# Attention with the queries on the partitions, in plain float32, ahead of two MoE layers

## The chip, the cores and the metric

The kernel runs on one core of a Trainium2 chip. The metric is the device time of one execution in microseconds (us). A difference of about 0.2% (2 us) is what a measurement of this kernel can tell from none.

## What is computed

The reference is a causal attention joined with a linear memory, and two feed-forward layers behind it. B = 4, H = 8, S = 576, D = 64, all in float32:

```python
scores = scale * np.matmul(q, k.transpose(0, 1, 3, 2))
...
a = np.exp(scores)
a /= a.sum(-1, keepdims=True) + 1e-09
local = np.matmul(a, v)
...
mem_ret = np.einsum('bhsd,bhde->bhse', q_p, M_prev)
mem_norm = np.einsum('bhsd,bhd->bhs', q_p, z_prev)[..., None] + 1e-06
mem_out = mem_ret / mem_norm
...
return (g * mem_out + (1 - g) * local).astype(np.float32)
```

Here q_p = phi(q), which is max(q, 0) + exp(min(q, 0)), and g is a sigmoid per head. The result, as x with 2304 rows of 512, goes through g(x @ w_in) @ w_out with a squared ReLU (d_ff = 2048), and then through a gated layer with d_ff = 1536.

## The kernel before

Every product is made at about float32 accuracy out of float32r parts: an operand is split into a rounded high part ("hi", ScalarE) and the rest ("lo", VectorE or GpSimd), and three products hi·hi, lo·hi and hi·lo are summed in PSUM.

The work is written as tasks with an engine, an assumed duration, an urgency from the table TUNE, the data they read and write, and the buffers that they take. The class Plan (line 41) runs a list scheduler over the tasks when the program is built, and its result is the order of each engine's instructions, which is then fixed. Buffer counts are in the table `slots`: PSUM has four banks of tag "s", one double bank of tag "w" and two banks of tag "h" in the first stage.

There are three stages. **The first** is 16 attention jobs (4 batches by 4 pairs of heads) and, between and behind them, the 128 chunks of h = x @ w_in (`h_mm`, line 313; 12 matmuls of 256 or 320 columns each). A chunk needs x of its batch and window (queries 0 to 255, or 256 to 575), so the first chunk needs the four jobs of batch 0. The weights w_in are decoded from 64-bit words (lines 248 to 275), 16 tiles with three VectorE steps each. **The second** is y = g @ w_out (`y_mm`, line 1048) and **the third** the gated layer (products m, line 1294, and the output o, line 1397).

One job, before:
- K and Q are transposed on TensorE (`transposed`, 5 + 5 blocks, line 416) and split into hi and lo (lines 480 to 504). The scores of five tiles of 128 queries are summed with the queries on the partitions (lines 626 and 652). VectorE adds the mask and finds the maximum (line 606), ScalarE takes the exponential and its row sum (line 668), and GpSimd multiplies P by the inverse sum (line 684).
- phi(q) is made with the queries on the partitions, normalised by z on VectorE and GpSimd (lines 519 to 551), transposed (`ft`) and split into hi and lo, stacked (lines 424 to 430). GpSimd splits V and M_prev (lines 404 to 407, 590 to 593).
- P is transposed in 25 blocks of 128x128 (`trans`, line 753), and each group is split: hi by ScalarE (line 776), lo by VectorE (line 780). The product (`pv`, lines 806 to 811) has V's hi and lo side by side as the stationary operand and the transposed P as the moving one, 64 to 320 columns, so that x comes out already transposed. The two halves are joined by ScalarE (line 830) and VectorE (line 834) in XB, and once a batch is whole it is split into hi and lo (lines 891 and 895).

Of the kernel before, what the change touches and what calls it, by code (L numbers as in the profile page):

```python
# [20 lines left out]
FB = 1  # L21
# [9 lines left out]
}  # L31
ENG = {"split": "DVE"}
# [118 lines left out]
def attention_moe_kernel(  # L151
# [18 lines left out]
    P = 128  # L170
# [166 lines left out]

    rawq = at.tile([P, NQ, P], F32, name="rawq", bufs=1)
    rawk = at.tile([P, NQ, P], F32, name="rawk", bufs=1)
    rawv = at.tile([P, NQ, P], F32, name="rawv", bufs=1)  # L340

    def zero_raw():


        for e in range(2):
            nc.gpsimd.memset(rawq[e * LAST : (e + 1) * LAST, NQ - 1, (1 - e) * D : (2 - e) * D], 0.0)
        nc.gpsimd.memset(rawk[LAST:, NQ - 1], 0.0)
        nc.gpsimd.memset(rawv[: P - LAST, NQ - 1], 0.0)
# [4 lines left out]
    iom = at.tile([P, NP, NC], F32, name="iom", bufs=1)  # L353

# [9 lines left out]
    def load_consts2():  # L364
        for e in range(2):
            c = slice(e * NQ, e * NQ + NT4)
            nc.vector.tensor_copy(iom[:, :, c], iomg[:, e::2].unsqueeze(2).broadcast_to([P, NP, NT4]))
            r = slice(e * LAST, (e + 1) * LAST)
            nc.vector.tensor_copy(iom[r, :, NT4], iomg[r, e::2])

    def load_raw(j, src, dst, ta):
        b, p, t0, t1 = jobs[j]
        te = min(t1, NQ - 1)
        d4 = dst.rearrange("p t (h d) -> p t h d", h=2)
# [17 lines left out]
    def load_mem(j):  # L392
        b, p = jobs[j][:2]
        h = slice(2 * p, 2 * p + 2)
        raw = T["mraw", j] = at.tile([P, 2, D], F32, tag="mraw", name=f"mraw{j}", bufs=1)
        for i in range(2):
            nc.sync.dma_start(raw[i * D : (i + 1) * D], M_prev[b, h].rearrange("h d e -> d h e"))
        z = T["z", j] = at.tile([P, 2, D], F32, tag="zbc", name=f"zbc{j}", bufs=1)
        nc.sync.dma_start(z, z_prev[b, h].partition_broadcast(P))

    def prep_m(j):
        raw = T.pop(("mraw", j))
        t = T["m", j] = at.tile([P, 2, 2, D], F32R, tag="mst", name=f"mst{j}")
        nc.gpsimd.tensor_scalar(
            out=t[:, :, 0], in0=raw, scalar1=1.0, scalar2=1.0, op0=ALU.mult, op1=ALU.mult
        )
        nc.gpsimd.tensor_tensor(out=t[:, :, 1], in0=raw, in1=t[:, :, 0].bitcast(F32), op=ALU.subtract)
# [14 lines left out]
    def stack_hi(t, ds):  # L422

        nc.scalar.copy(ds[0][:D], t[:D])
        nc.scalar.copy(ds[1][D:], t[D:])

    def stack_lo(t, ds):
        a, c = t[:D], t[D:]
        nc.vector.tensor_tensor(out=ds[0][D:], in0=a, in1=ds[0][:D].bitcast(F32), op=ALU.subtract)
        nc.vector.tensor_tensor(out=ds[1][:D], in0=c, in1=ds[1][D:].bitcast(F32), op=ALU.subtract)  # L430

    engine = {"DVE": nc.vector, "POOL": nc.gpsimd}
    slots = {
        "s": 4, "w": 1, "h": 2, "r": 2, "rawq": 1, "rawk": 1, "rawv": 1, "mem": 1, "mst": 2,
        "QT": 2, "KT": 2, "VHL": 2, "phi": 1, "phit": 1, "nrm": 2, "FS": 2, "P0": 3,
        "P1": 3, "P2": 3, "P3": 3, "P4": 1, "rs0": 2, "rs1": 2, "sums": 2, "PTA": 1, "PTB": 1,
        "PTC": 1, "XB": 1, "x0": 1, f"x{SPLIT}": 1, "raw": 2, "f": FB, "wt": 16,
# [8 lines left out]
    def mm(n):  # L446
        return max(108, 15 + n // 2.35)

# [6 lines left out]
    def plan_load(j):  # L455
# [4 lines left out]
        for src, dst, ta, key, du in (  # L460
            (q, rawq, t0, "rawq", AT["lq"]), (k, rawk, 0, "rawk", AT["lk"]), (v, rawv, 0, "rawv", AT["lv"]),
        ):
            add(
                "SP", 600 * ne, lambda src=src, dst=dst, ta=ta: load_raw(j, src, dst, ta), u + du,
                new=[(key, (key, j))], late=1900, size=(t1 - ta) * P * 800,
            )
        add("SP", 1800, lambda: load_mem(j), u + AT["lm"], new=[("mem", ("mem", j))], late=1900, size=1e5)

    def plan_prep(j):
# [8 lines left out]
        def q_hi():  # L478
            d = T["QT", j] = at.tile([P, 2, NQ * P], F32R, tag="QT", name=f"QT{j}")
            nc.scalar.activation(d[:, 0, t0 * P : t1 * P], T["qt", j], AF.Copy, scale=-SCALE)  # L480

        def q_lo():
            d, c = T["QT", j], slice(t0 * P, t1 * P)
            nc.vector.scalar_tensor_tensor(
                out=d[:, 1, c], in0=T.pop(("qt", j)), scalar=-SCALE, in1=d[:, 0, c].bitcast(F32),
                op0=ALU.mult, op1=ALU.subtract,
            )

        add("PE", 108 * nt, qt, u + AT["q"], reads=[("rawq", j)],
            new=[(bank(nt), ("qt", j)), ("QT", ("QT", j))], late=250)  # L490
        add("ACT", act(n), q_hi, u + AT["q"], reads=[("qt", j)], writes=[("QT", j)])
        add("DVE", dve(n), q_lo, u + AT["q"], reads=[("qt", j)], writes=[("QT", j)])


# [19 lines left out]
        def flat():  # L514
            return T["phi", j][:, t0:t1].rearrange("p t h d -> p (t h d)")

        def phi_a():
            T["phi", j] = at.tile([P, NQ, 2, D], F32, tag="phi", name=f"phi{j}", bufs=1)
            nc.scalar.activation(
                flat(), rawq[:, t0:t1].rearrange("p t d -> p (t d)"), AF.Relu, scale=-1.0  # L520
            )
            nc.scalar.activation(flat(), flat(), AF.Exp, scale=-1.0)

        def phi_b():
            nc.vector.scalar_tensor_tensor(
                out=flat(), in0=rawq[:, t0:t1].rearrange("p t d -> p (t d)"), scalar=0.0,
                in1=flat(), op0=ALU.max, op1=ALU.add,
            )

        def phi_z():  # L530
            tmp = at.tile([P, NQ, 2, D], F32, tag="phit", name=f"phit{j}", bufs=1)
            T["phit", j] = tmp = tmp[:, :nt]
            nc.gpsimd.tensor_tensor(
                out=tmp, in0=T["phi", j][:, t0:t1],
                in1=T.pop(("z", j)).unsqueeze(1).broadcast_to([P, nt, 2, D]), op=ALU.mult,
            )

        def phi_s():
            nrm = at.tile([P, NQ, 2], F32, tag="nrm", name=f"nrm{j}")
            T["nrm", j] = nrm = nrm[:, :nt]  # L540
            nc.vector.tensor_reduce(out=nrm, in_=T.pop(("phit", j)), axis=AX.X, op=ALU.add)
            nc.vector.scalar_tensor_tensor(
                out=nrm, in0=nrm, scalar=1e-6,
                in1=gt[:, 2 * p : 2 * p + 2].unsqueeze(1).broadcast_to([P, nt, 2]),
                op0=ALU.add, op1=ALU.mult,
            )
            nc.vector.reciprocal(nrm, nrm)

        def phi_n():
            u4 = T["phi", j][:, t0:t1]  # L550
            nc.gpsimd.tensor_tensor(
# [981 lines left out]
```

## Time and profile before

| | |
|---|---|
| times of the kernel before | 1090.67, 1091.19 and 1092.9 us, median 1091.19 |
| span of the profiled execution | 1090.0 us; no time of its own is listed beside it, so 1090.0 to 1091.19 is what it and the median differ by |
| busy share of the span | TensorE 95%, VectorE 70%, ScalarE 59%, GpSimd 55% |
| mean granted TensorE clock | 0.979 of 2.4 GHz |
| first chunk of h starts | 104.91 us |
| last of h ends, y follows | 462.8 us |
| third stage starts | 661.7 us |

A matmul's start is measured and its end modelled, so what one matmul costs in a stream is read here from the distance of starts, not from its mean duration, which has the pipeline's depth in it. Times of one execution count from the first instruction. PE is TensorE, DVE VectorE, ACT ScalarE and POOL GpSimd.

### The profile page before, as it was taken

The numbers are of one execution on the slowest core, as the hardware profiler recorded it, in microseconds if no ns is written. First come the engines' busy times: TensorE is split into PE (matmuls) and PEld (weight loads), VectorE is DVE, ScalarE is ACT, GpSimd is POOL, SyncE is SP. The second block draws the span as 40 slices with busy tenths as digits, with TensorE's granted clock in tenths as the row PEclk, the third lists the DMA queues.
The fourth block names the chain that finished last, engine by engine and source line by source line (L and its number), as shares of the span: only waits on it lengthen the run. The fifth ranks groups of instructions, "written<-read, shape, count | busy, mean of one in ns | idle before, by whom it ended". The sixth has DMA issues, their size and how long they took to land.

```text
span 1090.0 us, 18804 instructions
## 1 busy us (share of the span) xinstructions
PE 1040.3 (95%) x6496; PEld 977.0 (90%) x6496; DVE 766.3 (70%) x1434; ACT 647.6 (59%) x1407; POOL 598.4 (55%) x590
## 2 busy tenths in 40 slices
PE   4887998999999998999999999899999999999998
PEld 3676997899999998999999999898789998899986
DVE  5998987867667645777897765999726677266631
ACT  4877787787778656566666654565335453245421
POOL 5656666545434415474784554999427774177600
PEclk8877999999999999999999999999999999999999
DMA  5333554232323118868577776544214330133100
GB/s 135 80 82 81 170 145 120 72 85 81 106 85 92 47 61 264 259 204 267 174 245 262 261 268 221 183 160 160 87 63 136 113 125 29 63 119 118 69 24 35
DMA packets 135600, 145.95 MB, mean 134 GB/s; under 512 B 68176, under 2 KB 123472, under 8 KB 135504
## 3 DMA queue, kind: packets, MB, share of 16 engines
q1 hardware_dynamic: 135072, 144.74, 41.6%
q8 instruction: 51, 0.84, 0.3%
q14 instruction: 45, 0.37, 0.1%
q10 hardware_dynamic: 432, 0.01, 0.0%
HBM read 106.96 MB, written 37.75 MB: 133 GB/s over the span
## 4 chain that ended last, share of the span: by engine, by line
PE 80%; DVE 7%; POOL 7%; issue 2%; ACT 2%; DMA 1%; SPq 0%; DVEq 0%; POOLq 0%; ACTq 0%
PE m L1294 17%; PE h L319 17%; PE y L1057 16%; PE o L1397 14%; PE sc L626 3%; PE acc L806 3%; PE acc L807 2%; DVE set L1306 2%; PE pt_B L753 1%; PE sc L652 1%; POOL ws L1278 1%; POOL p L1316 1%; PE acc L810 1%; POOL w_out L271 1%; POOL P L684 1%
## 5 line engine op out<-in xcount | busy, mean ns | idle before, releaser
L1294 PE MATMUL m<-yt,ws 128*128 128x384 f32 x1512 | 264.5, 335 | 4.9 <-POOL ws L1278 3.5
L1294 PEld LDWEIGHTS m<-yt,ws 128*128 128x128 f32 x1512 | 262.0, 188 | 7.2 <-POOL ws L1278 4.7
L319 PE MATMUL h<-x,w_in 128*128 128x256 f32 (+1 forms) x1536 | 224.6, 300 | 5.5 <-POOL w_in L271 2.0
L319 PEld LDWEIGHTS h<-x,w_in 128*128 128x128 f32 x1536 | 207.8, 189 | 11.5 <-issue 3.7
L1306 DVE TENSOR_TENSOR set<-m,set 128x384 f32<-128x384 f32 x252 | 133.7, 554 | 57.8 <-PE m L1294 55.3
L1278 POOL TENSOR_TENSOR ws<-wf,ws 128x512 fp32r<-128x512 f32 (+1 forms) x108 | 124.7, 1175 | 86.4 <-ACT ws L1270 86.4
L1032 POOL TENSOR_SCALAR rr<-rr,sb_s,sb_b 128x384 f32<-128x384 f32 x96 | 103.8, 1088 | 96.7 <-ACT rr L1028 92.9
L1397 PE MATMUL o<-w_out,ps 128*128 128x512 f32 x648 | 154.0, 399 | 1.9 <-DVE ps L1387 1.5
L1397 PEld LDWEIGHTS o<-w_out,ps 128*128 128x128 f32 x648 | 122.7, 190 | 32.4 <-DVE ps L1387 2.3
L1057 PE MATMUL y<-gh,w_out 128*128 128x384 f32 x768 | 149.1, 335 | 2.4 <-ACT gh L1038 1.0
L1270 ACT CAST ws<-wf 128x512 fp32r<-128x512 f32 (+1 forms) x144 | 81.6, 568 | 103.4 <-PE m L1294 68.9
L1057 PEld LDWEIGHTS y<-gh,w_out 128*128 128x128 f32 x768 | 134.3, 188 | 3.3 <-ACT gh L1038 1.3
L1316 POOL TENSOR_TENSOR p<-set,set 128x384 f32<-128x384 f32 x72 | 85.7, 1214 | 40.9 <-DVE set L1306 40.9
L684 POOL TENSOR_SCALAR P<-P,rs 128x384 f32<-128x384 f32 (+3 forms) x144 | 85.2, 612 | 38.9 <-DVE rs L676 18.4
L1043 DVE TENSOR_TENSOR gl<-rr,gh 128x384 fp32r<-128x384 f32 x96 | 66.9, 701 | 51.5 <-PE y L1057 24.0
L606 DVE CUSTOM_DVE_ANT_0 P<-sc,mask 128x384 f32<-128x384 f32 (+2 forms) x144 | 70.5, 516 | 29.4 <-PE sc L626 13.6
L668 ACT ACTIVATE P<-P,nm 128x384 f32<-128x384 f32 (+2 forms) x144 | 83.8, 584 | 8.4 <-DVE nm L606 7.0
L329 ACT ACTIVATE r<-h 128x320 f32<-128x320 f32 (+1 forms) x128 | 52.3, 410 | 60.8 <-PE h L319 47.7
L1057 PE MATMUL y<-gl,w_out 128*128 128x384 f32 x384 | 82.0, 334 | 0.0
L1387 DVE TENSOR_TENSOR ps<-p,ps 128x512 fp32r<-128x512 f32 x54 | 47.4, 896 | 44.2 <-ACT ps L1374 44.2
L1374 ACT CAST ps<-p 128x512 fp32r<-128x512 f32 x54 | 32.5, 620 | 64.1 <-PE o L1397 50.6
L1038 ACT CAST gh<-rr 128x384 fp32r<-128x384 f32 x96 | 48.8, 511 | 33.2 <-PE y L1057 26.0
(134 smaller groups left out, 1712.1 us busy)
## 6 DMA issues: line engine op xcount, KB each, us to landing
wf<-weight_scratch SPq DMA_DIRECT2D x36, 896.0 KB, 4.5
rr<-relu_scratch SPq DMA_DIRECT2D x96, 192.0 KB, 3.7
raw_w_out<-in_moe_w_out_dram SPq DMA_DIRECT2D x28, 512.0 KB, 4.0
weight_scratch<-wm SPq DMA_DIRECT2D x12, 896.0 KB, 5.6
relu_scratch<-r SPq DMA_DIRECT2D x32, 320.0 KB, 2.3
raw_w_in<-in_moe_w_in_dram SPq DMA_DIRECT2D x16, 512.0 KB, 3.9
relu_scratch<-r SPq DMA_DIRECT2D x32, 256.0 KB, 2.3
raw_gv<-in_moe_w_gate_dram SPq DMA_DIRECT2D x12, 512.0 KB, 3.9
```

The costliest lines, as they stand in the source:

```text
L319: nc.tensor.matmul(t[:, :n], wt[:, wi, c], x[:, xi, c], start=(m == 0), stop=(m == 3 * NK - 1))
L606: nc.vector.tensor_tensor_reduce(out=pr, in0=ps, in1=mk, scale=1.0, scalar=3e38, op0=ALU.add, op1=ALU.min, accum_out=nm,)
L668: nc.scalar.activation(pr, pr, AF.Exp, bias=T.pop(("nm", j, e, t)), scale=-1.0, accum_out=T["sums", j][:, col : col + 1],)
L684: nc.gpsimd.tensor_scalar(out=pr, in0=pr, scalar1=T["rs", j, part][:, n : n + 1], scalar2=1.0, op0=ALU.mult, op1=ALU.mult,)
L1032: nc.gpsimd.tensor_scalar(out=r, in0=r, scalar1=sb_s, scalar2=sb_b, op0=ALU.mult, op1=ALU.add)
L1057: nc.tensor.matmul(accs[wi][d][:, :n], w_out_sb[f][:, x, d], y, start=(f == 0 and x == 0 and y is gh), stop=(f == NF - 1 and y is gl),)
L1270: nc.scalar.copy(t[:, 0, :m], flat(a, m))
L1278: engine[LOS[i]].tensor_tensor(out=t[:, 1, :m], in0=flat(a, m), in1=t[:, 0, :m].bitcast(F32), op=ALU.subtract)
L1294: nc.tensor.matmul(acc, wt[:, a, k : k + P], yt[:, y, c], start=(m == 0), stop=(m == 3 * K2 - 1),)
L1306: nc.vector.tensor_tensor(out=t[:, o], in0=Z["m", z, x], in1=t[:, i], op=ALU.add)
L1316: engine[TIMES[o]].tensor_tensor(out=p[:, f + HF * OF[o][0], OF[o][1]], in0=Z["set", z][:, o], in1=Z["set", zg][:, o], op=ALU.mult,)
L1397: nc.tensor.matmul(Z["zo", z], Z["ps", z, i][:, a, k * P : (k + 1) * P], w_out2_sb[f][:, x].rearrange("p c f -> p (c f)"), start=(i == k = ...
```

## The change

The reference's function stays the same, and so do the scores, the second stage and the third. In the attention job:
- The exponentials are no longer normalised and no longer summed by ScalarE. V gets a column of ones (`vals`, 66 wide of which 65 are used), is not split, and is the moving operand; the transposed P, copied out of PSUM once in plain float32 (`p_copy`, ScalarE, group D on VectorE), is the stationary one. Each of the 25 blocks of 128 keys gives one plain float32 matmul of 65 columns; the five of the last tile give two each, of 64 stationary columns. The output has the queries on the partitions, the row sum in column 64.
- phi(q) is made from the transposed q in PSUM, unsplit. Ten plain float32 matmuls of 65 columns (`mem`) multiply it by M_prev with z as a last column; eight of them use 64 rows of the array, for the two heads in turn. `mem_norm` divides.
- `norm` divides the attention's part, GpSimd adds the two (`join`), and x is transposed at the end in four blocks and two half blocks (`xt`), and split into hi and lo straight into x. For the last batch, x is first kept whole and split when it is complete.
- The tiles are scored in the order 0 and 1, 2, 3, 4; V is double buffered; the numbers of TUNE are others, and the assumed duration of a plain float32 matmul of n columns is 15 + 1.75 n ns.

```diff
     rawq = at.tile([P, NQ, P], F32, name="rawq", bufs=1)
     rawk = at.tile([P, NQ, P], F32, name="rawk", bufs=1)
-    rawv = at.tile([P, NQ, P], F32, name="rawv", bufs=1)
+    vals = [at.tile([P, NQ, 2, VW], F32, name=f"vals{i}", bufs=1) for i in range(2)]
...
+        t = T["m", j] = at.tile([P, VW], F32, tag="mem", name=f"mem{j}")
+        nc.sync.dma_start(t[:, :D], M_prev[b, h].rearrange("h d e -> (h d) e"))
+        nc.sync.dma_start(t[:, D : D + 1], z_prev[b, h].rearrange("h (d o) -> (h d) o", o=1))
-
-    def prep_m(j):
...
         def q_hi():
+            f = T["phi", j] = at.tile([P, NQ * P], F32, tag="phi", name=f"phi{j}")
+            c = slice(t0 * P, t1 * P)
+            nc.scalar.activation(f[:, c], T["qt", j], AF.Relu, scale=-1.0)
...
+        def phi_a():
+            f = T["phi", j][:, t0 * P : t1 * P]
+            nc.scalar.activation(f, f, AF.Exp, scale=-1.0)
...
+        def phi_b():
+            f = T["phi", j][:, t0 * P : t1 * P]
+            nc.vector.scalar_tensor_tensor(
+                out=f, in0=T.pop(("qt", j)), scalar=0.0, in1=f, op0=ALU.max, op1=ALU.add
+            )
...
-        def phi_z():
...
-        def phi_s():
...
-        def phi_n():
...
-        def ft():
...
-        def f_hi():
...
-        def v_split():
...
+        def mem():
+
+            f, z = T["phi", j], T["m", j]
+            both = [ret(e) for e in range(2)]
+            for i, t in enumerate(both[0][0]):
+                for e in range(2):
+                    r = slice(e * D, (e + 1) * D)
+                    if t < NT4:
+                        nc.tensor.matmul(
+                            both[e][1][:, i, : D + 1], f[r, t * P : (t + 1) * P], z[r, : D + 1],
+                            start=(i == 0), stop=(i == len(both[e][0]) - 1),
+                        )
...
+        def mem_norm():
+            x = T["MX", j] = at.tile([P, NC, D], F32, tag="MX", name=f"MX{j}")
...
+                nc.vector.tensor_tensor(
+                    out=x[:, c], in0=m[:, :, :D],
+                    in1=rs[:, c].unsqueeze(2).broadcast_to([P, len(ts), D]), op=ALU.mult,
+                )
...
-            nc.scalar.activation(
-                pr, pr, AF.Exp, bias=T.pop(("nm", j, e, t)), scale=-1.0,
-                accum_out=T["sums", j][:, col : col + 1],
-            )
-
-        def rsums(part, cols):
...
-        def norm(part, t):
...
+            nc.scalar.activation(pr, pr, AF.Exp, bias=T.pop(("nm", j, e, t)), scale=-1.0)
...
-        "B0": [(0, 4, S - P), (0, 2, 0), (0, 3, 0), (0, 4, 0)],
...
+        "B0": [(0, 2, k * P) for k in range(3)],
+        "B1": [(1, 2, k * P) for k in range(3)],
+        "C0": [(0, 3, k * P) for k in range(4)],
+        "C1": [(1, 3, k * P) for k in range(4)],
+        "D": [(0, 4, min(k * P, S - P)) for k in range(5)],
     }
+    WINS = {0: ["A0", "A1"], 1: ["B0", "B1", "C0", "C1", "D"]}
...
+        def p_copy(g):
...
+            if EVICT[g] == "ACT":
+                nc.scalar.copy(flat, ps)
+            else:
+                nc.vector.tensor_copy(flat, ps)
+
+        def pv(win, g):
...
+                    for i, k in ks:
+                        nc.tensor.matmul(
+                            o[r, c, : D + 1], pt[:, i, n], vt[:, k, h, : D + 1],
...
+        def norm(win):
...
+            nc.vector.reciprocal(rs[:, :nu], rs[:, :nu])
+            nc.vector.tensor_tensor(
+                out=x[:, :nu], in0=o[:, :, :D],
+                in1=rs[:, :nu].unsqueeze(2).broadcast_to([P, nu, D]), op=ALU.mult,
+            )
+
+        def join(win):
...
+            engine[ENG["join"]].tensor_tensor(
+                out=x[:, :nu], in0=x[:, :nu], in1=T["MX", j][:, 4 * win : 4 * win + nu], op=ALU.add
+            )
+
+        def xt(win):
...
+            for i in range(2):
+                nc.tensor.transpose(
+                    t[:, i * P : (i + 1) * P],
+                    x[:, 2 * i : 2 * i + 2].rearrange("p e d -> p (e d)"), ident,
+                )
...
+        def x_hi(win):
...
+            nc.scalar.copy(xw[b, c0][:, 0, p], T["xt", j, win][:, :n])
+
+        def x_lo(win):
...
+            nc.vector.tensor_tensor(
+                out=t[:, 1, p], in0=T.pop(("xt", j, win))[:, :n], in1=t[:, 0, p].bitcast(F32),
+                op=ALU.subtract,
+            )
...
-    TILES = [[2], [3], [4], [0, 1]]
-    NORM = [2, 3, 4, 0, 1]
+    TILES = [[0, 1], [2], [3], [4]]
```

`h_mm` itself is as before. Its tasks now also wait for the four parts of x by name.

On TensorE, where the fourth job's products end and the first chunk of h starts (acc is the output of `pv`, FS the split phi, PT the transposed P, x the input of h). Before:

```order
L807 MATMUL acc_1_0_1260<-PT_C,VHL_802 64x192
L806 MATMUL acc_1_0_1260<-PTB_1169,VHL_802 128x64
L807 MATMUL acc_1_0_1260<-PTB_1169,VHL_802 64x64
L810 MATMUL acc_1_0_1260<-FS_0_1104,mst_817 128x320
...
L810 MATMUL acc_1_1_1298<-FS_1_1105,mst_817 128x256
L810 MATMUL acc_1_1_1298<-FS_1_1105,mst_817 128x64
L319 MATMUL h_0_0_1319<-x_0_1296,w_in_136 128x256 x12
L319 MATMUL h_0_1_1337<-x_0_1296,w_in_145 128x256 x12
```

With the change (o and ret are the outputs of `pv` and `mem`, vals is V with ones, xt the transposed x):

```order
L689 MATMUL pt_B_1055<-ident,P_1_2_968 128x128 x3
L754 MATMUL xt_0_1063<-ident,X_0_1022 128x128 x2
L689 MATMUL pt_C_1074<-ident,P_0_3_1040 128x128 x4
L720 MATMUL o_1_1035<-vals_93,PT_B_1069 128x65 x3
L413 MATMUL qt_1087<-ident,rawq 128x128 x5
L720 MATMUL o_1_1035<-vals_93,PT_C_1083 128x65 x4
...
L539 MATMUL ret_0_1102<-mem_653,phi_875 64x65 x2
L689 MATMUL pt_C_1126<-ident,P_1_3_1059 128x128 x4
L320 MATMUL h_0_0_1131<-x_0_393,w_in_176 128x256 x12
L720 MATMUL o_1_1035<-vals_93,PT_C_1148 128x65 x4
```

The first chunk of h stood behind all products of the fourth job and behind the fifth job's scores; now it stands behind the first window's transposed x, ahead of the rest of the fourth job.

On VectorE, the part of a job from its second score tile to its last. Before (XB is the joined x, PTA to PTC the split P, nrm the norm of phi):

```order
L606 ISA P_1_2_676,nm_7_677<-sc_1_2_572,mask 128x384
...
L834 TENSOR_TENSOR XB_410<-acc_0_0_660,XB_410 64x256
L780 TENSOR_TENSOR PTB_619<-pt_B_671,PTB_619 128x384
L541 TENSOR_REDUCE nrm_708<-phit_666 128x10
L542 SCALAR_TENSOR_TENSOR nrm_708<-nrm_708,gt 128x10
L547 RECIPROCAL nrm_708<-nrm_708 128x10
L780 TENSOR_TENSOR PT_A_706<-pt_A_697,PT_A_706 128x384
L780 TENSOR_TENSOR PT_C<-pt_C,PT_C 128x384
L780 TENSOR_TENSOR PTB_619<-pt_D_712,PTB_619 128x2x256
L606 ISA P_1_3_734,nm_8_735<-sc_1_3_591,mask 128x512
...
L834 TENSOR_TENSOR XB_410<-acc_0_1_723,XB_410 64x256
L780 TENSOR_TENSOR PTB_619<-pt_D_730,PTB_619 128x256
```

With the change (ro and rm are inverse sums, X and MX the two parts of x):

```order
L733 SCALAR_TENSOR_TENSOR ro_1_747<-o_1_556,iom 128x5
L737 RECIPROCAL ro_1_747<-ro_1_747 128x5
L738 TENSOR_TENSOR X_1_746<-o_1_556,ro_1_747 128x320
...
L733 SCALAR_TENSOR_TENSOR ro_0_784<-o_0_759,iom 128x4
L737 RECIPROCAL ro_0_784<-ro_0_784 128x4
L738 TENSOR_TENSOR X_0_783<-o_0_759,ro_0_784 128x256
L510 TENSOR_TENSOR KT_781<-kt_740,KT_781 128x576
L576 ISA P_0_3_801,nm_3_802<-sc_0_3_773,mask 128x512
...
L776 TENSOR_TENSOR x_256_571<-xt_1_789,x_256_571 128x320
L576 ISA P_1_3_820,nm_8_821<-sc_1_3_774,mask 128x512
```

The subtractions into PT and the sums into XB are gone; two small operations and a multiplication per window stand in their place, and the subtraction into x is now made per job.

## Rows read from the trace of the kernel before

**Rows 1.** The page's first part: busy time, share and instructions of each engine.
```profile
PE 1040.3 (95%) x6496; PEld 977.0 (90%) x6496; DVE 766.3 (70%) x1434; ACT 647.6 (59%) x1407; POOL 598.4 (55%) x590
```

**Rows 2.** Busy us by stage of PE, PEld, DVE, ACT, POOL; then clock, DMA share, GB/s.
```profile
0.00:105.00 105.00, 76.58 (x458) 62.56 (x459) 86.58 (x209) 73.93 (x173) 61.87 (x86) 0.80 0.39 97
105.00:400.00 295.00, 288.27 (x2310) 273.63 (x2308) 219.84 (x540) 223.62 (x551) 148.38 (x186) 1.00 0.34 97
463.00:662.00 199.00, 198.00 (x1142) 197.68 (x1141) 146.94 (x239) 122.32 (x256) 116.74 (x98) 1.00 0.72 239
662.00:1090.00 428.00, 417.42 (x2160) 384.14 (x2158) 274.95 (x399) 191.66 (x350) 244.52 (x199) 1.00 0.30 105
```

**Rows 3.** The same view over three job periods, from the third job's q on.
```profile
41.28:102.20 60.92, 48.88 (x286) 40.94 (x286) 54.61 (x127) 47.33 (x114) 39.55 (x48) 0.72 0.33 84
```

**Rows 4.** TensorE in order of time, first stage: start, length, instruction.
```profile
61.74 0.76 PE L416 MATMUL qt<-ident,rawq 128*128 128x128 f32 x5
...
82.21 0.76 PE L416 MATMUL qt<-ident,rawq 128*128 128x128 f32 x5
...
104.91 3.58 PE L319 MATMUL h<-x,w_in 128*128 128x256 f32 x26
```

**Rows 5.** The longest wait of TensorE to 105 us: total, times, longest.
```profile
PE ft L416 <- DVE QT L484: 8.9, 4, 3.7
```

**Rows 6.** VectorE's groups to 463 us: count, busy us and mean ns, idle before.
```profile
L834 DVE TENSOR_TENSOR XB<-acc,XB 64x256 f32<-64x256 f32 (+2 forms) x80 | 29.7, 387 | 20.0 <-ACT XB L830 19.0
...
L429 DVE TENSOR_TENSOR FS<-ft,FS 64x640 fp32r<-64x640 f32 x16 | 13.1, 818 | 3.1 <-ACT FS L425 2.3
L541 DVE TENSOR_REDUCE nrm<-phit 128x10 f32<-128x640 f32 x16 | 13.0, 813 | 2.1 <-POOL phit L533 2.0
...
L676 DVE SCALAR_TENSOR_TENSOR rs<-sums,iom 128x5 f32<-128x5 f32 (+1 forms) x32 | 7.3, 229 | 5.1 <-ACT P L668 4.8
```

**Rows 7.** Busy time to 463 us of line 780 alone (windows).
```profile
0.00:463.00 463.00, 68.85 (x128) 0.96 0.40 116
```

**Rows 8.** VectorE's groups by shape: prices for the added operations.
```profile
L834 DVE TENSOR_TENSOR XB<-acc,XB 64x256 f32<-64x256 f32 x48 | 20.0, 416 | 13.7 <-ACT XB L830 13.1
...
L484 DVE SCALAR_TENSOR_TENSOR QT<-qt,QT 128x640 fp32r<-128x640 f32 x16 | 13.2, 822 | 5.4 <-ACT QT L480 5.3
...
L834 DVE TENSOR_TENSOR XB<-acc,XB 64x320 f32<-64x320 f32 x16 | 7.7, 482 | 6.4 <-ACT XB L830 5.9
```

**Rows 9.** TensorE in order of time between 310 and 323 us, at full clock.
```profile
310.02 0.31 PE L806 MATMUL acc<-PTB,VHL 128*128 128x320 f32 x1
...
311.12 0.22 PE L807 MATMUL acc<-PTB,VHL 128*64 128x64 f32 x1
311.18 0.39 PE L810 MATMUL acc<-FS,mst 128*128 128x320 f32 x1
311.41 0.71 PE L416 MATMUL qt<-ident,rawq 128*128 128x128 f32 x5
311.88 0.39 PE L806 MATMUL acc<-PTB,VHL 128*128 128x320 f32 x1
...
313.45 0.96 PE L626 MATMUL sc<-KT,QT 64*128 64x128 f32 x12
...
316.46 1.49 PE L626 MATMUL sc<-KT,QT 64*128 64x384 f32 x12
317.88 1.70 PE L319 MATMUL h<-x,w_in 128*128 128x256 f32 x12
...
319.88 3.12 PE L319 MATMUL h<-x,w_in 128*128 128x256 f32 x24
322.84 0.93 PE L753 MATMUL pt_B<-ident,P 128*128 128x128 f32 x7
```

**Rows 10.** TensorE's groups: the matmul with the most columns.
```profile
L1397 PE MATMUL o<-w_out,ps 128*128 128x512 f32 x648 | 154.0, 399 | 1.9 <-DVE ps L1387 1.5 <-ACT ps L1374 0.3
```

More of the change, by code (lines that the diff above doesn't have):

```diff
@@ L420, in bank @@
         return "s" if nt <= 4 else "w"
[L422 to L430, printed above, removed]
     engine = {"DVE": nc.vector, "POOL": nc.gpsimd}
     slots = {
[L434 to L437, printed above, removed]
[3 rows of a table added]
+        **{f"x{c0}_{i}": 1 for c0 in (0, SPLIT) for i in range(2)}, "f": FB, "wt": 16,
         "raw2": RAW2, "f2": FB, "w2": 16, "rr": RR, "gh": GG, "gl": GG, "yacc": 2,
@@ L634, in largest @@
         def largest(e, t):
-            if ("sums", j) not in T:
-                T["sums", j] = at.tile([P, NC], F32, tag="sums", name=f"sums{j}")
             n = keys(t)
@@ new lines, in pv @@
+        def pv(win, g):
+            vt = vals[j % 2]
+            first = g == WINS[win][0]
+            if first:
+                o = ps_s.tile([P, 512], F32, tag="s", name=f"o{j}_{win}")
+                T["o", j, win] = o[:, : (4 + win) * VW].rearrange("p (u w) -> p u w", w=VW)
+            o, pt = T["o", j, win], T.pop(("PT", j, g))
+            units = {}
+            for i, (e, t, k0) in enumerate(GROUPS[g]):
+                units.setdefault((e, t), []).append((i, (k0 + P - 1) // P))
+            for (e, t), ks in units.items():
+                for x in range(2 if t == NT4 else 1):
+                    if t < NT4:
+                        r, c, n, h = slice(0, P), 2 * (t - 2 * win) + e, slice(0, P), e
+                    else:
+                        r, c, h = slice(x * LAST, (x + 1) * LAST), 4, x
+                        n = r
+                    for i, k in ks:
+                        nc.tensor.matmul(
+                            o[r, c, : D + 1], pt[:, i, n], vt[:, k, h, : D + 1],
+                            start=first,
+                            stop=(g == WINS[win][-1] and (e, t) == list(units)[-1]
+                                  and i == ks[-1][0]),
+                        )
+                        first = False
@@ new lines, in s_hi, with s_lo @@
+        def s_hi(win):
+            c0, n = ((0, SPLIT), (SPLIT, BW))[win]
+            xf[win] = xw[b, c0]
+            t = xw[b, c0] = xpool.tile([P, 2, NP, n], F32R, tag=f"x{c0}", name=f"xl{c0}", bufs=1)
+            nc.scalar.copy(t[:, 0], xf[win][:, 0])
+        def s_lo(win):
+            c0, n = ((0, SPLIT), (SPLIT, BW))[win]
+            t = xw[b, c0]
+            nc.vector.tensor_tensor(
+                out=t[:, 1], in0=xf[win][:, 0], in1=t[:, 0].bitcast(F32), op=ALU.subtract
+            )
@@ L917, in plan_h @@
             "PE", 12 * mm(n), lambda: h_mm(b, c0, n, f), u,
-            reads=[("x", b, c0), ("wt", f)] + ([("hc", m - 1)] if m else []),
+            reads=[("x", b, c0), ("wt", f)] + [("xb", b, int(c0 > 0), pp) for pp in range(NP)] + ([("hc", m - 1)] if m else []),
             writes=[("hc", m)], new=[("h", ("h", m))], late=250,
```

414 lines of the change are left out of this document (148 added, 266 removed), and 15 rows, old and new, of tables (TUNE, slots).

## Prediction

> **What bounds the kernel now.** I read the page's engine shares first: TensorE is busy for 95% of the span and no other engine comes near it [rows 1]. A mean hides the stages, so next come the windows. From 463 us on TensorE is idle for 1.0 of 199 us and 10.6 of 428 us [rows 2]. The change touches no instruction's work there, so I carry that part over whole. In the first stage two regimes are to be seen. Up to 105 us TensorE is busy for 76.6 us at a mean granted clock of 0.80, that is, partly at the lower of its two levels (1.2 and 2.4 GHz); from 105 to 400 us it is busy for 288.3 of 295 us at full clock [rows 2]. So the opening is bound by something else, and the rest by TensorE.
>
> What bounds the opening is seen over three job periods: VectorE is busy for 54.6 of 60.9 us, ScalarE for 47.3, GpSimd for 39.6 [rows 3]. A job starts every 20.47 us (61.74 to 82.21) [rows 4], and 54.6 / 3 = 18.2 us of it is VectorE at work. TensorE's longest wait there is for VectorE, 8.9 us in total before the phi transposes [rows 5]. The first chunk of h, which needs four jobs, starts at 104.91 us [rows 4].
>
> So the change is worth two things: how much sooner four jobs are through, which VectorE sets, and what a job costs TensorE afterwards, when TensorE is full.
>
> **VectorE, per job.** Removed: line 780, 68.85 / 16 = 4.30 us [rows 7]; the sums into XB, 29.7 / 16 = 1.86; the stacking of phi, two rows like the one shown, 1.64; the reduction for z, 0.81, and its two small operations at 0.2 each [rows 6]. That is 9.0 us. Added, by shape [rows 8]: in the division of the memory part two multiplications from PSUM of 320 and 256 columns, 0.48 + 0.42 (the row of 320 and of 256 columns, whose partition count should not matter), with three small operations at 0.23 or less [rows 6], 1.56 together; the division of the two windows, 0.42 + 0.48 (its four small operations take the place of the four on the row sums); the subtractions into x, 0.42 + 0.48, while the batch's large split goes; the copy of group D, 640 columns, 0.82 as Q's split. That is 4.2 us. Net -4.8: 18.2 becomes 13.4 us a job. ScalarE loses the phi stacking and the row sums, GpSimd the scaling of P and the splits; both had less to do than VectorE before [rows 3] and are no nearer to the bound after.
>
> **The opening.** Four jobs at 13.4 us are 54 us of VectorE. Up to 105 us it is now idle for 105 - 86.6 = 18.4 us, filling included [rows 2]; I keep that, which gives 72 us. The order adds two small things: the first chunk of h stands ahead of the fourth job's last products, but behind the next job's q. A shallower pipeline (less of a next job lies ahead) makes for more waits in fixed queues, so I take 75 us, with 68 and 90 as ends: **-30 us**. TensorE will by then have done less of what it had done at 105 us: the fifth job's scores, some 3 us (twelve of them take 1.42 us, 316.46 to 317.88 [rows 9]; the rest, of fewer columns, about as much again), and some 1.5 us of the fourth job's products: **+4.5 us**.
>
> **TensorE, per job, at full clock [rows 9].** Removed: the two products of the second window take 1.39 us (310.02 to 311.41) and 1.57 us (311.88 to 313.45); the first window has 2048 of their 5504 columns, 1.10 us; five phi transposes, at the rate of the q's (5 in 0.47 us, 94 ns each), 0.47. Together 4.53 us. P still has 25 transposes and the scores stay. Added: 30 plain float32 products of 65 columns with P, 10 with phi, and `xt`, four transposes at 94 ns and two halves, 0.5 us.
>
> No row shows a plain float32 product. From below, the float32r one of 64 columns starts 60 ns before its successor (311.12 to 311.18) [rows 9]; from above, the largest matmul in the kernel, 512 columns, takes 154.0 / 648 = 238 ns [rows 10]. The nearest relative is the transpose, whose operand is plain float32: 94 ns for 128 columns, against 123 ns for 256 float32r columns ((322.84 - 319.88) / 24) [rows 9], so about 1.5 times as much per column. There only one operand needs full width, here both do; I charge each column four times, 260 columns, and so take the row of 256 columns, **123 ns**. Eight of the products with phi use half the rows each, and so do the scores, whose 12 matmuls of 384 and 512 columns (5376 in all) take 1.42 us or 0.26 ns per column, against 123 / 256 = 0.48 for h: pairs overlap. I count those eight at half. So 32 x 0.123 + 8 x 0.062 + 0.5 = 4.93 us, +0.4 a job, and for the 12 jobs behind the first chunk **+5 us**. The four before it lie in VectorE's shadow as long as a job takes TensorE less than 13.4 us. Now it takes 48.9 / 3 = 16.3 us at a clock of 0.72, about 12 at full clock [rows 3]; I take it that the clock holds once TensorE has more to do, as it does from 105 us on [rows 2].
>
> The Trainium skill (FP8 and Floating Point Precision, TensorE Precision Notes) says that a true FP32 product takes four passes through the array; four times 65 columns at 2.4 GHz are an estimate of 108 ns, by which the sum would be some 6 us lower. No run here shows it yet.
>
> **Waits afterwards.** From 105 to 400 us TensorE idles for 6.7 us [rows 2]. With VectorE and GpSimd lighter I expect half: **-3 us**. The order of the second and third stage is drawn anew by other numbers; its idle 11.6 us [rows 2] could grow or shrink by some 5 us; I count nothing and put it into the range. It also has the cover that decoding w_out needs: more chunks of h (54, not 35) stand behind the last attention instruction.
>
> **Sum.** -30 + 4.5 + 5 - 3 = -23.5. The profiled execution's span is 1090.0 us, 1.2 below the median of the three runs; from the median, 1091.2 - 23.5 gives **1067.5 us**.
>
> **Rivals.**
> - *The plain product is dear (slower).* If each of the 40 costs like the largest row, 238 ns (pairs 119), a job costs TensorE 32 x 0.238 + 8 x 0.119 + 0.5 = 9.1 us in place of 4.5, +4.5 where I have +0.4, so +50 us over 12 jobs; and a job in the opening takes TensorE about 16 us, over VectorE's 13.4, for another +6. That gives 1124 us. It ends in a loss from about 177 ns on (23.5 / (12 x 36) = 54 ns above my price). For it: TensorE is full behind 105 us, so nothing hides it. Against: a 128-column weight load in float32r fits into 60 ns [rows 9], so a stream of columns is the likelier limit. Chance 0.16. The Trainium skill (TensorE: Matmul & The Clock Gate, LDWEIGHTS and Weight-path perf modes) speaks for this one: it gives a load of 128 columns as 128 / 1.2 = 107 ns and has no fast load for FP32. Two such loads per product, for a high and a low part, would be an estimate of 213 ns and a time of about 1110 us. The float32r row differs from that figure; for plain float32 no row decides.
> - *The opening shrinks less.* kt, qt, the last tile's scores and group D all pass through the one double bank, and qt is now held until ScalarE has gone over it three times and VectorE twice. If such waits make a job 19 us rather than 15, or the clock stays at 0.72 and TensorE's 16.3 us a job [rows 3] become the bound with waits on top, the first chunk starts at about 91 us: 1083 us. For it: 20.47 us a job against 18.2 of work is what waits cost already [rows 3, 4]. Chance 0.14.
> - *The plain product is cheap.* At 70 ns (near the lower end) 12 jobs save 12 x 36 x 0.053 = 23 us more: 1044 us. Chance 0.10.
>
> **How the numbers follow.** The forecast itself has 0.60, and its own range, by the ends of the opening (68 and 90) and the later stages, is 1055 to 1083. The range reaches down past the cheap product to 1040, and up to 1100, which takes in the weaker opening and a product of up to about 195 ns; some 0.05 lies below and 0.13 above. A measurement of this kernel tells about 0.2%, 2 us, from no change. Faster: nearly all of the forecast, the cheap product, most of the weak opening, 0.78; within 0.2%: 0.03; slower: 0.19, the dear product and a bad tail of the opening.
>
> **What would show it.** The first chunk of h near 75 us, jobs in the opening every 15 us, and VectorE there with about 13.4 us of work a job; starts of the products with P 110 to 135 ns apart; the last of h near 440 us; the later stages 627 us long, as now. I am wrong if the products stand 180 ns or more apart, if the first chunk starts later than 90 us, or if the time won by 440 us is given back behind it.

## The result and the profile after

The changed kernel takes **1105.2 us** (median of 4 runs, 1104.42 to 1107.51) against 1091.32 us before: ratio 1.0128, 95% interval 1.0108 to 1.0147. It is slower, where I forecast 1067.5 us. The profiled execution has a time of 1104.42 us and a span of 1102.6 us.

Page of the change, first part, beside [rows 1]:

```profile
PE 1074.9 (97%) x7296; PEld 1011.8 (92%) x7296; DVE 658.4 (60%) x1296; ACT 579.3 (53%) x1145; POOL 438.1 (40%) x385
```

VectorE, ScalarE and GpSimd lost 108, 68 and 160 us of work; TensorE, which was full already, gained 35 us and 800 instructions. Where they went is seen in the windows of the change, cut at its own events (columns as in [rows 2]): up to the first h, one job period within that, from the first h to 400 us, the second stage, and the third.

```profile
0.00:81.89 81.89, 68.79 (x608) 59.65 (x609) 50.77 (x165) 50.92 (x97) 13.67 (x28) 0.96 0.41 100
59.35:78.69 19.34, 18.66 (x156) 16.30 (x155) 12.25 (x39) 11.90 (x24) 3.16 (x3) 0.82 0.31 75
81.89:400.00 318.11, 317.95 (x2853) 296.93 (x2852) 152.06 (x450) 173.66 (x358) 37.53 (x38) 1.00 0.31 86
477.34:676.21 198.87, 198.06 (x1142) 197.54 (x1141) 152.19 (x246) 125.36 (x259) 120.73 (x99) 1.00 0.74 243
676.21:1102.00 425.79, 414.88 (x2161) 383.47 (x2160) 273.38 (x399) 191.64 (x351) 243.44 (x199) 1.00 0.31 105
```

The first h comes at 81.89 us, 23.0 earlier than before [rows 4]. From there to the third stage, whose first m starts at 676.21 us, TensorE is busy nearly all of the time, and this stretch is 594.3 us long; before it was 661.70 - 104.91 = 556.8. So 37.5 us are lost in it. The third stage takes 426.4 us to the end of the span, before 428.3. Together -23.0 + 37.5 - 1.9 = +12.6, the difference of the spans.

The loss stands in TensorE's timeline of the change. A row gives start, length and instruction; then the stationary operand, which is loaded first (`128*64` is 128 rows by 64 columns), the moving one, which is streamed past it (`128x65` has 65 columns), and the count:

```profile
277.74 1.20 PE L720 MATMUL o<-vals,PT_D 128*64 128x65 f32 x20
278.87 0.87 PE L689 MATMUL pt_A<-ident,P 128*128 128x128 f32 x6
279.58 0.71 PE L413 MATMUL kt<-ident,rawk 128*128 128x128 f32 x5
280.13 0.78 PE L720 MATMUL o<-vals,PT_A 128*128 128x65 f32 x6
280.84 0.79 PE L596 MATMUL sc<-KT,QT 64*128 64x384 f32 x6
```

A plain float32 product is two instructions: three products of PT_A are x6, and the 10 of PT_D x20. Each instruction has a weight load of its own (the page counts 7296 of both). Three products with 128 stationary columns (128*128) take 280.84 - 280.13 = 0.71 us, ten with 64 (128*64) only 278.87 - 277.74 = 1.13 us. For a price I take, over all rows of a tile from 100 to 400 us, the distance from a row's start to the next row's and divide by the instructions; rows followed by a wait are left out. That gives **110 ns** an instruction, 219 ns a product, where the block of P has 128 queries (456 instructions, 50.00 us), and 57 ns, 113 a product, for the last tile with 64 (240 instructions, 13.59 us). The weight loads (PEld) say the same: within a tile they start 112 ns apart for 128 stationary columns and 58 for 64 (medians of 396 and 228).

### The profile page after: what moved, and what is told of

The parts are those of the page before. It is cut to its first block, busy times and chain, and to the rows that moved or that the text cites. A ratio compares the mean times of both kernels' runs of the same rounds, so it can differ in the third digit from the quotient of the medians.

```text
span 1102.6 us, 19715 instructions
## 1 busy us (share of the span) xinstructions
PE 1074.9 (97%) x7296; PEld 1011.8 (92%) x7296; DVE 658.4 (60%) x1296; ACT 579.3 (53%) x1145; POOL 438.1 (40%) x385
## 4 chain that ended last, share of the span: by engine, by line
PE 87%; POOL 6%; DVE 2%; DMA 2%; issue 2%; ACT 1%; SPq 0%; POOLq 0%; DVEq 0%; ACTq 0%
PE h L320 18%; PE m L1241 17%; PE y L1004 17%; PE o L1344 13%; PE o L720 8%; PE sc L596 4%; POOL ws L1225 3%; POOL p L1263 2%; PE ret L533 2%; PE sc L620 1%; PE pt_C L689 1%; PE pt_A L689 1%; POOL w_out L272 1%; PE pt_B L689 1%; PE kt L413 1%
## 5 line engine op out<-in xcount | busy, mean ns | idle before, releaser
L320 PE MATMUL h<-x,w_in 128*128 128x320 f32 (+1 forms) x1152 | 169.6, 300 | 0.0
L320 PEld LDWEIGHTS h<-x,w_in 128*128 128x128 f32 x1152 | 155.8, 189 | 2.8 <-issue 1.6
L979 POOL TENSOR_SCALAR rr<-rr,sb_s,sb_b 128x384 f32<-128x384 f32 x96 | 106.9, 1121 | 112.4 <-ACT rr L975 107.4
L746 POOL TENSOR_TENSOR X<-X,MX 128x256 f32<-128x256 f32 (+1 forms) x32 | 27.0, 843 | 265.6 <-DVE X L738 195.1
L576 DVE CUSTOM_DVE_ANT_0 P<-sc,mask 128x128 f32<-128x128 f32 (+4 forms) x144 | 68.8, 516 | 50.0 <-PE sc L596 44.0
L636 ACT ACTIVATE P<-P,nm 128x128 f32<-128x128 f32 (+4 forms) x144 | 80.0, 584 | 33.4 <-DVE nm L576 33.3
L990 DVE TENSOR_TENSOR gl<-rr,gh 128x384 fp32r<-128x384 f32 x96 | 61.1, 638 | 46.2 <-ACT gh L985 26.8
L1004 PEld LDWEIGHTS y<-gl,w_out 128*128 128x128 f32 x384 | 67.9, 188 | 0.2 <-DVE gl L990 0.2
L975 ACT ACTIVATE rr<-rr 128x384 f32<-128x384 f32 x96 | 49.0, 522 | 30.7 <-DMA rr<-relu_scratch 30.3
```

The costliest lines, as they stand in the source:

```text
L320: nc.tensor.matmul(t[:, :n], wt[:, wi, c], x[:, xi, c], start=(m == 0), stop=(m == 3 * NK - 1))
L576: nc.vector.tensor_tensor_reduce(out=pr, in0=ps, in1=mk, scale=1.0, scalar=3e38, op0=ALU.add, op1=ALU.min, accum_out=nm,)
L636: nc.scalar.activation(pr, pr, AF.Exp, bias=T.pop(("nm", j, e, t)), scale=-1.0)
L979: nc.gpsimd.tensor_scalar(out=r, in0=r, scalar1=sb_s, scalar2=sb_b, op0=ALU.mult, op1=ALU.add)
L1004: nc.tensor.matmul(accs[wi][d][:, :n], w_out_sb[f][:, x, d], y, start=(f == 0 and x == 0 and y is gh), stop=(f == NF - 1 and y is gl),)
```

## The experiments

**Theory L:** an instruction costs at least the load of its stationary columns, and a plain float32 product loads them twice. Rivals: S, the price is that of streaming the moving columns; F, a fixed price for each instruction; O, the loss comes from something else in the stage. After e2 comes theory A: instructions on different halves of the array overlap. The diffs are shortened; `...` stands for what is left out.

All results together. The kernel before, timed again beside each group of runs, took 1091.0 to 1092.0 us (medians). First h and first m are from the profiled executions; the prices are for one instruction of a product of P and V, worked out as above (e9 and e10 from 110 us). The expectations below carry 109, 55 and 37.5 ns for 110, 57 and 38; no reading hangs on the difference.

| kernel | time us | ratio to before (95%) | first h us | first h to m us | 128 queries, ns | last tile, ns |
|---|---|---|---|---|---|---|
| before | 1091.3 | | 104.91 | 556.8 | | |
| the change | 1105.2 | 1.0108 to 1.0147 | 81.89 | 594.3 | 110 | 57 |
| e1, 33 columns moved | 1121.81 | 1.0239 to 1.0309 | 97.16 | 595.3 | 108 | 55 |
| e2, halves by turns | 1090.17 | 0.9974 to 0.9993 | 75.81 | 584.2 | 38 | 55 |
| e3, float32r | 1074.95 | 0.9817 to 0.9865 | 77.89 | 568.5 | 118 | 57 |
| e4, told costs | 1111.13 | 1.0154 to 1.0198 | 85.52 | 597.0 | 112 | 57 |
| e5, halves apart | 1102.13 | 1.0065 to 1.0115 | 78.06 | 594.2 | 49 | 50 |
| e6, all halves by turns | 1083.38 | 0.9892 to 0.9946 | 74.09 | 579.4 | 38 | 35 |
| e7, 100 columns moved | 1112.49 | 1.0161 to 1.0211 | 81.15 | 600.9 | 112 | 79 |
| e8, float32r, last tile by turns | 1067.17 | 0.9738 to 0.9807 | 72.12 | 564.2 | 118 | 37 |
| e9, M's heads apart | 1135.83 | 1.0359 to 1.0450 | 91.19 | 611.2 | 110 | 57 |
| e10, e6 with told costs | 1086.54 | 0.9917 to 0.9964 | 80.29 | 577.6 | 38 | 35 |

**e1: half of the moving columns.**

```diff
-    o[r, c, : D + 1], pt[:, i, n], vt[:, k, h, : D + 1],
+    o[r, c, D // 2 : D + 1], pt[:, i, n], vt[:, k, h, D // 2 : D + 1],
```

> The products of P and V (L720) move columns 32 to 64 of V and the column of ones, 33 columns in place of 65; stationary operand, number and order of the instructions stay. The other 32 columns of the local output are left out (those of the right half stand in their place; one more small instruction on DVE writes them). Theory L, the price of a plain float32 product is that of loading its stationary columns twice: the eight instructions of four products of PT_C still stand 0.93 us apart, and the time stays at 1105 us, give or take 3. Rival S, the price is that of streaming the moving columns several times: half of it goes, 20 products of 0.22 us and 10 of 0.11 us a job over 12 jobs are 66 us, so about 33 less: 1072 us. Rival F, a fixed price for each instruction: no change, as with L.

The price stayed: 108 and 55 ns. First h to m is 1.0 us longer. S falls; L and F stand. The whole time, though, grew by 16.6 us, which none had foreseen, and 15.3 of it lie before the first h. The windows of e1 from 20 to 40 and 40 to 60 us:

```profile
20.00:40.00 20.00, 18.47 (x164) 16.70 (x162) 13.62 (x44) 12.57 (x25) 1.97 (x2) 0.83 0.33 72
40.00:60.00 20.00, 19.62 (x101) 16.86 (x101) 8.80 (x26) 8.76 (x17) 1.98 (x2) 0.50 0.20 51
```

From 40 to 60 us the granted clock is 0.50, the lower level (1.2 GHz) throughout, with TensorE busy for 19.62 of 20 us; it gets through 101 instructions there. In the change the same window shows 1.00 and 185. So e1's extra time goes with the clock of the opening; why the clock stayed low there isn't shown.

**e2: the stationary block in two halves, by turns.**

```diff
     for i, k in ks:
-        nc.tensor.matmul(o[r, c, : D + 1], pt[:, i, n], ...)
+        for y in range(2 if t < NT4 else 1):
+            m = slice(y * D, (y + 1) * D) if t < NT4 else n
+            nc.tensor.matmul(o[m, c, : D + 1], pt[:, i, m], ...)
```

> Each product of P and V with 128 stationary columns is issued as two with 64 stationary columns each (queries 0 to 63, then 64 to 127 of the block), with the same 65 moving columns; the result is the same. Theory L: a product of 64 stationary columns took 0.113 us in the trace, so two of them take what one of 128 took, and the time stays at 1105 us, give or take 5. Rival F, a fixed price of about 0.11 us for each instruction: 20 more products a job of 0.22 us over 12 jobs are 53 us more, 1158 us. Rival S, streaming moving columns: 65 columns are streamed twice as often, the same 53 us more.

None of the three foresaw this: twice the instructions, the same arithmetic, and 15 us less. F falls, and L alone isn't enough. Timeline of e2, four products of PT_C as 16 instructions, then the last tile, untouched:

```profile
240.39 0.69 PE L722 MATMUL o<-vals,PT_C 128*64 128x65 f32 x16
240.91 1.15 PE L722 MATMUL o<-vals,PT_D 128*64 128x65 f32 x20
241.99 0.96 PE L596 MATMUL sc<-KT,QT 64*128 64x128 f32 x12
```

The 16 take 0.52 us, 33 ns each; the 20 of the same shape behind them 1.08 us, 54 ns each. Shape doesn't tell them apart; order does. In PT_C the halves alternate, in PT_D five products of head 0 come first and then five of head 1. Not all of the low price is gain: from first h to m these products take 17.0 us less, but the stretch fell by 10.1. Rows next to them rose (pt_C's transposes from 109 to 117 ns, h of 256 columns from 127 to 130). A change of shape has a price: from a start with 128*128 to the first 128*64 behind it 203 ns pass, on the way out 152 (medians, 100 to 400 us). e2 makes this passage 53 times in and 62 out, the change 11 and 12. Inside a run two instructions, one on each half, take 58 ns together, which is what one alone takes in PT_D.

**e3: float32r, one instruction per large product.**

```diff
-    t = T["PT", j, g] = at.tile([P, n, P], F32, ...)
+    t = T["PT", j, g] = at.tile([P, n, P], F32 if g == "D" else F32R, ...)
...
-    vt = vals[j % 2]
+    vt = (vals if g == "D" else valr)[j % 2]
```

> The 20 products a job with 128 stationary columns take P and V rounded to float32r, one product each in place of the plain float32 one; the low parts are left out. The ten products of the last tile of queries stay in plain float32. POOL rounds V, one more instruction a job. Theory that the loss is the price of these products (L, or S): one float32r product takes 60 ns or less, as the weight loads of 128 columns in the kernel before, so 240 products save 0.16 us each, 38 us: about 1067 us, and the first h still starts near 82 us. Rival O, the loss comes from something else in stage one (order of the work, evictions, transposes of x at the end): the time stays above 1095 us.

O falls: with half the instructions for these products, 25.8 us of first h to m are gone, 107 ns for each of 240. But the float32r product takes 118 ns, not 60. Timeline of e3:

```profile
251.52 0.61 PE L730 MATMUL o<-valr,PT_C 128*128 128x66 f32 x4
252.06 1.11 PE L535 MATMUL ret<-mem,phi 64*128 64x65 f32 x16
```

Four in 0.54 us, 135 ns each here. Its weight loads start 111 ns apart (median of 169), those of plain float32 112. An instruction with 128 stationary columns costs about the same in either type; plain float32 needs two of them.

**e4: the planner is told the measured prices.**

```diff
 def mm4(n):
-    return 15 + 1.75 * n
+    return 225
...
```

> The costs by which the planner orders the work are set to what the trace showed: 225 ns for each product of P and V and 260 ns for each pair of products with M, in place of 129 ns for each and for each pair. The instructions are the same, only their order moves. If the loss is the products' price on a full TensorE, an order cannot give it back: 1105 us, give or take 6. Rival O, the order planned with a wrong cost is what loses: 1095 us or less.

It is 5.9 us slower than the change. In the profiled execution, the slowest of its four, the first h comes 3.6 us later, first h to m is 2.7 longer and the third stage 3.0. The wrong costs in the plan are not what loses.

**e5: the halves apart.** As e2, with the loops over halves and blocks exchanged:

```diff
-    for i, k in ks:
-        for y in range(2 if t < NT4 else 1):
+    for y in range(2 if t < NT4 else 1):
+        for i, k in ks:
```

> As e2, each product of P and V issued as two with 64 stationary columns, but first the lower halves of all blocks of a tile, then their upper halves, so that neighbours nearly always write the same half of the output's partitions. In e2, where the halves alternate, one instruction took 37.5 ns on average from start to start (34 ns in PT_C), against 55 ns in PT_D, whose halves follow one another in fives. Theory A, instructions on different halves of the array overlap: without the alternation each takes 53 to 55 ns, four of them 215 to 220 ns a product, as the unsplit product of the change: 20 x 12 x 0.07 us = 17 us more than e2, 1105 us, give or take 5. Rival, smaller loads are simply cheaper whatever their order: as e2, 1090 us.

49 ns in place of 38 on average, and first h to m is back at 594.2 us, as in the change (594.3). Against e2 the stretch grew by 10.0 us and these products by 9.8; the rows next to them cost what they do in e2, so their rise belongs to the shape and not to the order. So a smaller load isn't cheaper for its columns, and the gain of e2 hangs on neighbours that use different halves: A holds. On one half instructions start 58 ns apart, and only where the halves change do a few overlap; where a tile has few blocks and they change often, the price is lower (PT_A 43 ns, PT_B 53).

**e6: the last tile by turns too.**

```diff
-    for x in range(2 if t == NT4 else 1):
-        ...
-        for i, k in ks:
+    for i, k in ks:
+        for y in range(2):
+            m = slice(y * D, (y + 1) * D)
```

> As e2, and the ten products a job of the last tile of queries (PT_D) alternate their halves too (head 0 into the lower, head 1 into the upper, block by block). Theory A: their 20 instructions go from 55 to about 37 ns, 0.36 us a job, 12 jobs, 4 us: 1086 us, give or take 2, faster than both kernels. Rival: nothing to gain there, 1090 us.

The 20 instructions of the last tile in e6:

```profile
236.39 0.75 PE L717 MATMUL o<-vals,PT_D 128*64 128x65 f32 x20
237.07 0.95 PE L596 MATMUL sc<-KT,QT 64*128 64x128 f32 x12
```

They fell from 55 to 35 ns each, first h to m by 4.8 us, the whole by 6.8. This version does all products in plain float32, as the change does, and **beats both kernels**: 0.9919 of before.

**e7: 100 moving columns.**

```diff
-    VW = D + 2
+    VW, OW = D + 2, 100
...
+    s0 = min((2 * k + h) * VW, 2 * NQ * VW - OW)
...
-    o[r, c, : D + 1], pt[:, i, n], vt[:, k, h, : D + 1],
+    o[r, c], pt[:, i, n], vt.rearrange("p q h w -> p (q h w)")[:, s0 : s0 + OW],
```

> The products of P and V move 100 columns in place of 65 (the 65 that are used and 35 neighbours whose results nobody reads; for one block of the last 64 queries of odd heads the columns are the wrong ones). Theory L: an instruction still takes 109 ns, since the load of 128 columns is longer than the moving; after the first h the time is that of the change, within 3 us. Rival S, streaming of moving columns: 35 more of 65, 54% of 7.8 us of products with 128 and 64 stationary columns a job, over 12 jobs some 40 us more. On the opening: e1 with 33 columns lost its 16 us there, where the clock was granted at half for longer. If that comes from the fewer columns moved, the first h stands at 82 us or earlier here, and the whole at 1105 us or less; if the clock there is settled by something else, the first h may stand anywhere from 76 to 97 us.

With 128 stationary columns the price is 112 ns, against 108 with 33 and 110 with 65 columns moved. With 64 it rose from 57 to 79 ns, and that is 20 x 12 x 22 ns = 5.3 us of the 6.6 by which first h to m grew, where L had allowed 3; S asked for far more (at the measured 5.5 us a job, not 7.8, some 36 us). So where neighbours use the same half, an instruction takes the longer of its load and its streaming; with 65 columns moved, the load decides for a block of 128 queries, and for 64 the two are about equal. The clock was 1.00 in every window up to 100 us, and the first h stood at 81.15.

**e8: e3 and the turns of e6 for the last tile.** Beside the diff of e3:

```diff
+    for y in range(2 if t == NT4 else 1):
+        m = slice(y * D, (y + 1) * D) if t == NT4 else slice(0, P)
```

> As e3 (P and V of the 20 large products a job rounded to float32r, their low parts left out), and the ten plain float32 products of the last tile alternate their halves as in e6. Theory A: 4 us less than e3: 1071 us, give or take 2. Rival: as e3, 1075 us.

4.3 us of first h to m came from the last tile as foreseen; another 5.8 came in the opening, so that the time is below the range expected. It is the fastest version, with the accuracy given up that e3 gives up.

**e9: the products with M, one head after the other.**

```diff
-    for i, t in enumerate(both[0][0]):
-        for e in range(2):
+    for e in range(2):
+        for i, t in enumerate(both[0][0]):
```

> The changed kernel, but the products of phi(q) with M_prev and z are issued for all tiles of one head first and then for all of the other, in place of by turns. One head's lie in partitions 0 to 63 of the array's rows, the other's in 64 to 127. By turns one instruction (64 rows, 128 stationary columns) took 65 ns from start to start, less than the 109 ns of a load of 128 columns over all rows. Theory A, instructions on different halves of the array overlap, in rows as in columns: without the turns each takes about 107 ns, 16 x 0.042 us x 12 jobs = 8 us: 1113 us, give or take 3. Rival, a load of 64 rows is cheaper by itself: no change, 1105 us.

Timeline of the change, and then of e9:

```profile
80.17 1.11 PE L533 MATMUL ret<-mem,phi 64*128 64x65 f32 x16
81.22 0.33 PE L539 MATMUL ret<-mem,phi 64*64 64x65 f32 x4
```

```profile
241.77 1.10 PE L533 MATMUL ret<-mem,phi 64*128 64x65 f32 x8
242.80 0.33 PE L539 MATMUL ret<-mem,phi 64*64 64x65 f32 x2
243.06 1.10 PE L533 MATMUL ret<-mem,phi 64*128 64x65 f32 x8
```

By turns 16 instructions take 1.05 us, apart 8 take 1.03: 65 and 129 ns each. Halves of rows overlap entirely; I had expected 107 ns apart. That is 16 x 64 + 4 x 66 ns = 1.3 us a job; 11 jobs' products with M stand behind the first h, 14 us of the 16.9 by which first h to m grew. A further 9.3 us lie before the first h, at a granted clock of 0.83 from 40 to 80 us. So the time grew by 30.6 us, where 8 had been expected.

The 129 ns are not the price of a load. The weight loads of 64 rows and 128 columns start 111 ns apart within a head (median of 154), about as those of 128 rows; the rest lies at the end of each run, where from a start with 64*128 to the first 64*64 behind it 202 ns pass (median of 22). Apart, a job makes this passage twice.

**e10: e6 with its measured prices in the plan.**

```diff
 def mm4(n):
-    return 15 + 1.75 * n
+    return 150
...
```

> As e6 (all products of P and V in alternating halves), and the planner's costs are set to what e6 took: 150 ns for a product of P and V with 128 queries, 144 ns for a block of the last tile, 260 ns for a pair of products with M. The instructions are the same, their order moves. With TensorE full after the first h the order can move only the time up to it: 1083 us, give or take 4. Rival: a true cost in the plan gives 5 us or more either way.

3.2 us slower than e6, with ratios whose intervals overlap: the first h 6.2 us later, first h to m 1.8 us shorter. The order moves the opening most, and no rule for it came out of e4 and e10.

## Why the prediction was wrong

**The step that failed** is the price: "I charge each column four times, 260 columns, and so take the row of 256 columns, 123 ns". A job's products on TensorE, forecast and measured:

| per job | forecast us | measured us |
|---|---|---|
| 20 products with 128 queries | 20 x 0.123 = 2.46 | 20 x 0.219 = 4.39 |
| 10 of the last tile | 1.23 | 10 x 0.113 = 1.13 |
| 10 with M | 0.74 | 20 instructions x 0.065 = 1.30 |
| `xt` | 0.5 | 4 x 0.140 + 4 x 0.065 = 0.82 |
| sum | 4.93 | 7.64 |

2.71 us a job too little, over 12 jobs 32.5 us; the stretch from the first h to m was forecast at +4.5 + 5 - 3 = +6.5 and came out at +37.5, 31.0 more. The mis-sized term covers the miss. Summed from start to start over all of TensorE's instructions in this stretch, the new products and `xt` take 93.3 us, where 60.7 had been counted (12 x 4.93, and 1.5 of the fourth job). The other terms came out near: what was removed had taken 56.1 us (12 x 4.53 = 54.4 forecast), the waits fell by 7.7, and what both kernels do there takes 8.0 us more, of it 5.1 for scores (30 instructions more, the fifth job's) and 3.1 for P's transposes. The experiments that change these products alone move the stretch by as much as the products: e3 by 25.8 us (products 24.8), e5 against e2 by 10.0 (9.8), e6 against e2 by 4.8 (5.2).

Streaming was not absurd as a price: for 64 queries a product takes 113 ns where I had 123. For 128 the load is longer, and it was dismissed with "a 128-column weight load in float32r fits into 60 ns [rows 9], so a stream of columns is the likelier limit". That was a misreading. The instruction that starts 60 ns before its successor, at 311.12 us, has 64 stationary columns (128*64). The weight loads of the kernel before, at the same place, show what the 60 ns are:

```profile
310.99 0.19 PEld L806 LDWEIGHTS acc<-PTB,VHL 128*128 128x128 f32 x1
311.09 0.14 PEld L807 LDWEIGHTS acc<-PTB,VHL 128*64 128x64 f32 x1
311.15 0.19 PEld L810 LDWEIGHTS acc<-FS,mst 128*128 128x128 f32 x1
311.29 0.14 PEld L416 LDWEIGHTS qt<-ident,rawq 128*128 128x128 f32 x1
```

From start to start, the load of 128 columns at 310.99 takes 108 ns and the load of 64 at 311.09 takes 57; the load for the successor, 128 columns from 311.15 on, has the next behind it only at 311.29. From 100 to 400 us of the kernel before, none of the 1424 loads of 128*128 for h, the scores and `pv` has the next behind it in less than 108 ns. So the price of a load stood in the trace before the change, and the row that was taken to rule it out agrees with it. e3's expectation of 60 ns took over the same misreading.

The rival "the plain product is dear" is what happened. Its 238 ns was near the 219 of the large products, its 1124 us too much, mostly because it charged the last tile alike. The Trainium skill (TensorE: Matmul & The Clock Gate, LDWEIGHTS) has the load go by columns, P / 1.2 in ns, an estimate of 107 ns for 128; the runs agree where the load decides, 108 to 112 ns for 128 columns and 55 ns for 64 (e1), two of them a product. The prediction's estimate from it, 213 ns and about 1110 us, was the nearest figure that I had, and I gave this rival 0.16 against a single row, misread.

**The opening** was right in kind and too large: -23.0 in place of -30. VectorE's work came out near the forecast, 12.25 us in the period from 59.35 to 78.69 us (forecast 13.4). What failed is the condition on TensorE, that the four jobs "lie in VectorE's shadow as long as a job takes TensorE less than 13.4 us": in that period TensorE is busy for 18.66 of 19.34 us. The bound passed from VectorE to TensorE, by the same price. The clock, which I took to hold, fell to 0.82 there; the period before it, 42.80 to 59.35 us, with nearly the same instructions (155 for 156) at 1.00, is 16.55 us long. In e6, with cheaper products and a clock of 1.00, the first h stands at 74.09 us; 75 had been forecast.

**The waits** after the first h went from 6.7 us to 0.16 (up to 400 us), 6.5 less where I had 3. **The third stage** kept its length within 1.9 us, inside the 5 allowed. **Pairs on half the rows overlap**, which I had read from the scores, was right, and e9 shows it directly.

## What to carry to other kernels

A plain float32 matmul is two instructions, each at least as long as the load of its stationary columns where neighbours use the same half of the array; with few moving columns count the stationary ones, about 0.9 ns each (112 ns for 128, 58 for 64), twice. Issued in halves of 64 stationary columns by turns, the same products made the change faster than the kernel before: 22 us here, 15 of them from first h to m and most of the rest in the opening. Going over from one shape to another costs, so long runs of one shape should gain most, which no run tried. And read the price of a load from the distance of load starts (PEld): the distance of two matmul starts can hold the load of another shape.

## What was not expected of the hardware

- Two instructions on different column halves overlap: 35 to 40 ns by turns (e2), 51 to 53 where they follow on one half in PT_B and PT_C (e5); inside a run a pair takes the 58 ns of one. The Trainium skill (TensorE: Matmul & The Clock Gate, The mechanism) has loads overlap with running matmuls only where the row group differs; here the rows are the same and the columns differ, and the time falls all the same.
- Halves of rows overlap entirely, 65 against 129 ns (e9), and a load over 64 rows takes as long as one over 128: 111 and 112 ns from start to start.
- Where the stationary shape changes around the new products, 149 to 205 ns pass from start to start (medians in the change, e2, e5 and e6: 203 to 205 into 128*64, 152 out of it, 201 to 202 from 64*128 to 64*64, 149 out of that), against 58 or less inside a run of 128*64. In the kernel before, whose products are float32r, it is 130 and 118 ns between 128*128 and 128*64. Why isn't shown.
- The clock in the opening differs from kernel to kernel while TensorE is busy nearly throughout: 0.50 from 40 to 60 us in e1, 0.83 in e9, 1.00 in e2, e6 and e7. It goes with the kernel and not with the execution: the mean granted clock is 0.972 to 0.981 in e1's four executions and 0.997 to 0.998 in e2's ten. What decides it stays open. With it, in e1, the first h came 15 us later than in the change.
